# Query features and attention sums of the later groups: sixteen 32x32 tiles of TensorE, or four 64x64 tiles with a pair of heads in each

## The chip, the cores and the metric

One core of a Trainium2 chip runs the whole kernel. The metric is device time in microseconds (us), taken as the median of several runs. Beside it stands the profile of one execution.

## What is computed

A linear attention with polynomial features, followed by a two-layer feed-forward block with ELU, all in 32-bit floats:

```python
a = einsum('rd,bhsd->bhsr', S1, x); b = einsum('rd,bhsd->bhsr', S2, x)   # r = 8
phi(x) = outer(a, b)                          # 64 features
kv  = einsum('bhsf,bhsd->bhfd', phi(k), v);   z = phi(k).sum(over s)
num = einsum('bhsf,bhfd->bhsd', phi(q), kv)
den = einsum('bhsf,bhf->bhs', phi(q), z) + 1e-06
x   = (num / den) as 4352 tokens x 128        # 4 batches x 1088, 4 heads x 32
h   = x @ w_in                                # 128 -> 2048
out = where(h > 0, h, exp(min(h, 0)) - 1) @ w_out   # 2048 -> 128
```

## The kernel before, in words

**Groups and steps.** The 4352 tokens are 68 half tiles of 64 tokens (17 of each batch), taken in nine groups: eight of 512 tokens (8 half tiles) and a last one of 256. For each group the 2048 hidden channels are worked off in 8 pairs of 128 channels (`cp`). A pair of a group is a step; the list `steps` (L837) holds 72 of them: groups 0 and 1 share steps 0 to 15, then each group has eight steps in a row (2 from step 16, 3 from 24, 4 from 32 and so on).

**One step.** The loop at L925 writes out the order of every engine by hand; no planner reorders it. In step n TensorE makes h (`mm1`, records at L219) in two PSUM banks, then what `extra` holds for the step, then the second product of step n - 2: `o` for groups 0 and 1 (`mm2`, L219), `pa` and `pb` for groups 2 to 7 (`mm2_seven`, L668, seven products in place of eight, on sums `tt` that POOL makes), `ol` for the last group. ACT makes the exponential of h (L729, L731), DVE joins both into `gg` (L737), which lets go of the h bank. Four PSUM banks carry h, so a step's banks are those of the step two before. Two more banks have the tag `aux` and are shared by whatever comes up; the last two take o, pa and pb. The product of a step thus has two steps' time for ACT, DVE and POOL.

**Products in tiles.** TensorE is used in tiles. `halves` (L217) splits a product into two column halves (128x64 tiles). `KF_late` (L309), key features, uses eight 64x32 tiles. Every product of 32-bit floats shows as two records of TensorE, and two weight loads.

**Queries of the later groups.** Groups 2 to 8 get their x while the steps run. They are taken in units (L479): groups 2 and 3 alone, groups 4 and 5, 6 and 7 as pairs, and 8 alone. `un` is half of a unit's half tiles: 4, 4, 8, 8 and 2. For a unit the following happens, at the steps listed at L894:
- `q1` (L494) projects q with `SWq`, which holds for each batch and head the 32x32 block of S1, S2 and z (the last 8 columns are zero). It runs in sixteen 32x32 tiles: head h is the row of tiles, and c, a quarter of the unit's tokens, is the column. Head h writes bank h.
- `q1_out` (L504): four DVE transposes, one for each bank, put tokens on partitions (`abw`).
- `q2_den`, `q2_half` (L517, L572): division by the denominator and the outer product (DVE). `q4` (L580): DVE transposes features back onto partitions (`qpT`).
- `q5` (L587) multiplies with `kvq`, in two halves f of the features, again in sixteen 32x32 tiles: quarter c is the row of tiles and writes bank c, head h is the column.
- `q5_out` (L599): ACT copies x into `xg`, the input of mm1.

`parts` (L482) cuts a quarter where a batch ends inside it; the rest of the quarter then is a product of its own, and the products are sorted so that the rests come last. This occurs in units 2, 4 and 6.

`queries` (L609) runs at steps 13, 15, 22, 30, 46 and 62 and joins q5 of one unit with q1 of the next: q5 for f = 0, q1, q5 for f = 1. It takes four banks: the two h banks of the next step, ahead of that step's mm1, and both aux banks. x takes columns 0 to 255 of each, the features columns 256 to 511. q5_out and q1_out stand in the middle of the same step (`mid`), for a pair of groups the second q5_out at its end (`late`), so that mm1 of the next step can write the h banks.

**What feeds them.** `make_SWq` (L271, POOL, step 2) writes S1 and S2 into SWq for each batch, `Z_share` (L389, POOL) adds z of the batch when its keys are done, and `KV_out` (L399, DVE) copies the batch's sums from PSUM into kvq. `bmask` (L205) has a one for each channel at its head.

Of the kernel before, what the change touches and what calls it, by code (L numbers as in the profile page):

```python
# [12 lines left out]
F32 = mybir.dt.float32  # L13
# [9 lines left out]
def _ap(ap: bass.AP, free):  # L23
    return dataclasses.replace(ap, ap=[list(ap.ap[0])] + [list(x) for x in free])
# [3 lines left out]
def kernel(  # L28
# [21 lines left out]
    nc = tc.nc  # L50
    B, H, S, D = q.shape
    R = S1.shape[0]
    P = 128
    FD = H * D
# [9 lines left out]
    const = ctx.enter_context(tc.tile_pool(name="const", bufs=1))  # L64
    work = ctx.enter_context(tc.tile_pool(name="wk", bufs=2))
    psum = ctx.enter_context(tc.tile_pool(name="psum", bufs=2, space=bass.MemoryType.PSUM))
# [6 lines left out]
    qT = [const.tile([FD, NT, 64], F32, name=f"qT{b}") for b in range(2)] * 2  # L73
# [125 lines left out]
    for b in range(B):  # L199
        nc.gpsimd.memset(vt[b][64:, :VN].rearrange("p (h t d) -> p h t d", h=H, t=KT)[:, :, KT - 1, :], 0.0)  # L200
        if b < 2:
# [3 lines left out]
    bmask = const.tile([FD, H], F32, name="bmask")  # L205
# [2 lines left out]
    nc.vector.tensor_reduce(zmask[:].rearrange("p g i -> p (g i)"),  # L208
                            ident[:].rearrange("p (x j) -> p x j", j=R), axis=AX, op=ADD)

    hmask = const.tile([P, H], F32, name="hmask")
    nc.vector.tensor_reduce(hmask[:], _ap(zmask[:], [[1, H], [H, 4]]), axis=AX, op=ADD)

# [8 lines left out]
    def keep_warm(n, cols=256):  # L222
        for i in range(n):
            nc.tensor.matmul(idle[:, :cols], some[:, :P], some[:, :cols], skip_group_check=True)  # L224
# [26 lines left out]

    Sab = const.tile([FD, H, 2 * R], F32, name="Sab")
    SW = const.tile([FD, H, 3, R], F32, name="SW")
    SWq = const.tile([FD, B, 4, R], F32, name="SWq")
    keep_warm(3)
    keep_warm(1, 96)
    sps = psum.tile([P, 512], F32, name="sps", tag="aux")
# [7 lines left out]
    Sxp = const.tile([FD, 2, 2, R], F32, name="Sxp")  # L265
# [3 lines left out]
                             Sab[:, 2:].rearrange("p c (x r) -> p c x r", x=2))  # L269

    def make_SWq():  # L271
        nc.gpsimd.memset(SWq[:, :, 3, :], 0.0)
        for b in range(B):
            nc.gpsimd.tensor_add(SWq[:, b, :2, :], Sxp[:, :, 0, :], Sxp[:, :, 1, :])


    def outer(dst, ab, eng=nc.vector):
# [7 lines left out]
    kvq = const.tile([P, B, 2, H, D], F32, name="kvq")  # L285
# [102 lines left out]

    def Z_share(b):  # L389
        z = wzs.pop(b)  # L390
        zp = work.tile([FD, 2, R], F32, name="zp", tag="zp")
        nc.gpsimd.tensor_add(zp[:], z[:, :2], z[:, 2:])
        nc.gpsimd.tensor_add(SWq[:, b, 2, :], zp[:, 0], zp[:, 1])

    def KV(b, ps):
        for f in range(2):
            halves(ps[:, 128 + P * f:128 + P * f + P], kvz[b][:, f].rearrange("p c s -> p (c s)"), ident[:])

    def KV_out(b, ps):  # L399
        nc.vector.tensor_copy(kvq[:, b].rearrange("p f h d -> p (f h d)"), ps[:, 128:384])  # L400


    def Z_first():
# [14 lines left out]
    def KV_first():  # L418
        ps = psum.tile([P, 512], F32, name="kvps", tag="aux")
        KV(0, ps)  # L420
        KV_out(0, ps)
# [3 lines left out]
    NQ = (NH + 7) // 8  # L425
    qn = [min(8, NH - 8 * g) // 2 for g in range(NQ)]
    abw, ans, qp, qpT, xg, xps = {}, {}, {}, {}, {}, {}
# [4 lines left out]
    def half_tile(g, k):  # L432
        return divmod(8 * g + k, NT)
# [45 lines left out]
    units = {g: ([g, g + 1] if 4 <= g < NQ - 1 else [g]) for g in [2, 3] + list(range(4, NQ, 2))}  # L479
    un = {g: sum(qn[x] for x in gr) for g, gr in units.items()}  # L480

    def parts(g, c):  # L482

        n = un[g] // 2
        k = 0
        while k < n:
            b, t = half_tile(g, n * c + k)
            m = min(n - k, NT - t)
            yield b, t, k, m
            k += m  # L490

    def q1(g, ps, start=True):  # L494
        todo = [(j, c, h, x) for c in range(4) for h in range(H) for j, x in enumerate(parts(g, c))]
        for j, c, h, (b, t, k, m) in sorted(todo, key=lambda x: x[0]):
            r = slice(D * h, D * h + D)
            nc.tensor.matmul(ps[h][32 * c:32 * c + 32, 256 + 64 * k:256 + 64 * (k + m)],
                             SWq[r, b].rearrange("p x r -> p (x r)"),
                             qT[b][r, t:t + m, :].rearrange("p t s -> p (t s)"), start=start and j == 0, stop=True,  # L500
                             skip_group_check=True, tile_position=(D * h, 32 * c))
        abw[g] = ps

    def q1_out(g):  # L504
        ps, n = abw[g], un[g]
        pair = n > 4
        abw[g] = work.tile([P, H * n if pair else H * 4, 4 * R], F32, name="abw", tag="abwp" if pair else "abw",
                           bufs=1 if pair else 2)
        for h in range(H):
            nc.vector.transpose(abw[g][:, n * h:n * h + n, :].rearrange("p m y -> p (m y)"),  # L510
                                ps[h][:, 256:256 + 32 * n])

    def q2(g, parts=1):
        q2_den(g)
        q2_out(g, parts)
# [17 lines left out]
    def q2_out(g, parts=1):  # L533
        m = H * qn[g]
        x, an = abw.pop(g), ans.pop(g)
        qp[g] = work.tile([P, 4 * H, R, R], F32, name="qp", tag="qp", bufs=2)
        for i in range(parts):
            h = slice(i * m // parts, (i + 1) * m // parts)
            a_ = an[:, h]
            b_ = x[:, h, :R]  # L540
            nc.vector.tensor_mul(qp[g][:, h], _ap(a_, list(a_.ap[1:]) + [[0, R]]),  # L541
                                 _ap(b_, [b_.ap[1], [0, R], b_.ap[2]]))
# [26 lines left out]
    def heads(g):  # L569
        return 2 if un[g] > 4 else H  # L570
# [15 lines left out]

    def q5(g, ps, f):  # L587
        n = un[g]
        todo = [(j, h, c, x) for h in range(H) for c in range(4) for j, x in enumerate(parts(g, c))]
        for j, h, c, (b, t, k, m) in sorted(todo, key=lambda x: x[0]):  # L590
            i, o = divmod(h, heads(g))
            r = slice(32 * c, 32 * c + 32)
            nc.tensor.matmul(ps[c][D * h:D * h + D, 64 * k:64 * (k + m)], kvq[r, b, f, h, :],  # L593
                             qpT[g, i][r, n * o + 2 * k:n * o + 2 * (k + m), f, :],
                             start=(f == 0 and j == 0), stop=(f == 1),
                             skip_group_check=True, tile_position=(32 * c, D * h))
        xps[g] = ps

    def q5_out(g, i=0):  # L599

        ps, n, gr = xps[g], 32 * un[g], units[g]
        x = xg[g + i] = work.tile([P, 512], F32, name="xg", tag="xg", bufs=3)
        cs = range(4 // len(gr))
        for c in cs:

            o = n * c if g < NQ - 1 else n * (2 * (c % 2) + c // 2)
            nc.scalar.copy(x[:, o:o + n], ps[c + len(cs) * i][:, :n])

    def queries(g5, g1, n):  # L609

        hs[steps[n]] = [psum.tile([P, 512], F32, name="h", tag="h", bufs=4) for c in range(2)]
        ps = hs[steps[n]] + [psum.tile([P, 512], F32, name="qps", tag="aux") for _ in range(2)]

        if g5 is not None:
            q5(g5, ps, 0)
        if g1 is not None:
            q1(g1, ps, g5 is None)
        if g5 is not None:
            q5(g5, ps, 1)


    hs, es, gs, ops = {}, {}, {}, {}
# [214 lines left out]
    steps = [(0, 0), (0, 1), (1, 0), (1, 1)] + [(g, cp) for cp in range(2, NP) for g in range(2)]  # L837
# [19 lines left out]

    late(2, make_Sxp)
    late(2, make_SWq)
    late(3, Z_share, 0)  # L860
    late(3, KC, 0)
    late(8, KV_first)
# [10 lines left out]
    def turned(b):  # L873
        Z_out(b, kv_ps[b])
        KV_out(b, kv_ps[b])
        Z_share(b)
# [17 lines left out]
    for n, g, nx in ((13, None, 2), (15, 2, 3), (22, 3, 4), (30, 4, 6), (46, 6, 8), (62, 8, None)):  # L894
        at(n, queries, g, nx, n + 1)
        if g is not None:
            mid(n, q5_out, g)
        if nx is not None:
            mid(n, q1_out, nx)
        if g is not None and len(units[g]) > 1:  # L900
            late(n, q5_out, g, 1)
# [23 lines left out]
    for n in range(2, N + 2):  # L925
        if n < N:
            g, cp = steps[n]
# [26 lines left out]
        g, cp = steps[n - 2]  # L954
# [39 lines left out]
```

## Time and profile before

| | us |
|---|---|
| runs before, median of 5 | 269.46 |
| lowest and highest | 268.44 and 270.56 |
| the profiled execution | 270.49 |
| its span, first to last instruction | 268.7 |
| TensorE busy in the span | 262.3 |
| DVE, ACT, POOL busy | 189.7, 182.1, 166.0 |

The span is what the profile sees; the profiled execution's own time has some 1.8 us more around it. "PE" is TensorE's products and "PEld" its weight loads, which can lie beside them. A line such as `133.99 0.41 PE L593 MATMUL h<-qpT,kvq 32*32 32x128 f32 x2` in the timeline gives start and length in us, the line of the code, the tile written and those read, the rows and columns of the TensorE tile, rows by columns of the streamed operand, and how many records were merged. The recorded length of a product holds the way through the array (a 32x64 one has 0.22 us, a 32x256 one 0.39), so starts tell more than lengths. In the chain of what ended last, each line has start, length and the work that held the end at that time. In a table of stretches, each line has the bounds, the length, then the busy time of PE, PEld, DVE, ACT and POOL with numbers of instructions, the granted clock, the DMA share and GB/s.

### The profile page before, as it was taken

To read this page: it belongs to the slowest core of one execution; us is meant where nothing else is said; L and a number is where in the kernel's file an instruction comes from. 1 tells how busy PE (TensorE), PEld (TensorE's weight loads), DVE (VectorE), ACT (ScalarE), POOL (GpSimd) and SP (SyncE) were. 2 spreads that over 40 slices of the span, in tenths; PEclk is the share of its full clock that TensorE was granted. 3 is DMA by queue.
4 is the path that set the end of the run, shared out by engine and by line. 5 is a ranking of instruction groups with operands and counts; after the bars stand their busy time and mean duration, and the time that the engine had idled before them with its cause. 6 is when DMAs were issued, how large, how long until landed. Compare 5 with 4: busy or idle time off the path is not lost.

```text
span 268.7 us, 8155 instructions
## 1 busy us (share of the span) xinstructions
PE 262.3 (98%) x3343; PEld 157.0 (58%) x3343; DVE 189.7 (71%) x350; ACT 182.1 (68%) x351; POOL 166.0 (62%) x233
## 2 busy tenths in 40 slices
PE   8899999999999999999999999999999999999994
PEld 5853333343343666666676666666766666666884
DVE  6599999996969896997658667464347444673652
ACT  2368978685565656676667766777777767677782
POOL 4500006402506996699979999988698889897300
PEclk9999999999999999999999999999999999999999
DMA  6997882002001300000200110001001100110021
GB/s 190 310 348 197 233 223 47 0 2 83 2 2 29 53 4 2 2 2 11 31 7 0 16 27 2 2 11 23 10 4 15 28 1 2 17 16 12 2 29 32
DMA packets 26420, 13.63 MB, mean 51 GB/s; under 512 B 19216, under 2 KB 24592, under 8 KB 26384
## 3 DMA queue, kind: packets, MB, share of 16 engines
q1 hardware_dynamic: 25792, 12.66, 19.6%
q8 instruction: 26, 0.43, 0.7%
q10 hardware_dynamic: 592, 0.46, 0.5%
q14 instruction: 10, 0.08, 0.1%
HBM read 10.88 MB, written 2.23 MB: 49 GB/s over the span
## 4 chain that ended last, share of the span: by engine, by line
PE 88%; DVE 6%; POOL 2%; issue 1%; ACT 1%; DVEq 0%
PE h L219 40%; PE pb L668 15%; PE pa L668 12%; PE o L219 9%; PE ol L219 3%; PE h L593 2%; PE idle L224 2%; PE kv L365 1%; DVE gg L737 1%; DVE qp L541 1%; PE abp L296 1%; POOL kp L280 1%; PE kfps L315 1%; POOL tt L651 1%; PE kv L219 1%
## 5 line engine op out<-in xcount | busy, mean ns | idle before, releaser
L737 DVE SCALAR_TENSOR_TENSOR gg<-e,h 128x512 f32<-128x512 f32 (+1 forms) x144 | 92.3, 651 | 63.2 <-ACT e L731 58.4
L219 PE MATMUL h<-xg,W 128*64 128x512 f32 (+1 forms) x584 | 128.7, 563 | 0.0
L729 ACT ACTIVATE e<-h 128x512 f32<-128x512 f32 (+1 forms) x144 | 81.5, 566 | 56.0 <-PE h L219 55.1
L731 ACT ACTIVATE e<-e 128x512 f32<-128x512 f32 (+1 forms) x144 | 87.5, 607 | 4.4
L219 PEld LDWEIGHTS h<-xg,W 128*64 128x64 f32 x584 | 40.2, 137 | 47.3 <-issue 36.8
L651 POOL TENSOR_TENSOR tt<-gg 128x256 f32<-128x256 f32 x48 | 39.2, 818 | 11.1 <-DVE gg L737 10.7
L648 POOL TENSOR_TENSOR tt<-gg 128x256 f32<-128x256 f32 x48 | 35.1, 732 | 14.5 <-DVE gg L737 14.3
L653 POOL TENSOR_TENSOR tt<-gg,tt 128x256 f32<-128x256 f32 x48 | 38.5, 801 | 3.8
L652 POOL TENSOR_TENSOR tt<-tt,gg 128x256 f32<-128x256 f32 x48 | 36.0, 749 | 3.8
L668 PEld LDWEIGHTS pa<-gg,W 128*64 128x64 f32 x384 | 23.6, 137 | 22.6 <-issue 22.0
L219 PE MATMUL o<-gg,W 128*64 128x512 f32 x128 | 30.5, 597 | 0.4 <-DVE W L125 0.4
L668 PE MATMUL pa<-gg,W 128*64 128x128 f32 x384 | 29.5, 275 | 0.0
L668 PE MATMUL pb<-tt,SS 128*64 128x128 f32 x384 | 29.1, 273 | 0.0
L668 PEld LDWEIGHTS pb<-tt,SS 128*64 128x64 f32 x384 | 22.7, 137 | 0.0
L122 POOL TENSOR_TENSOR raw<-raw,tiny 128x512 f32<-128x512 f32 x1 | 1.0, 1042 | 29.6 <-DVE raw L117 29.6
L668 PE MATMUL pa<-tt,SS 128*64 128x128 f32 x192 | 18.7, 273 | 0.2 <-POOL tt L652 0.2
L668 PE MATMUL pb<-gg,SS 128*64 128x128 f32 x192 | 18.7, 273 | 0.0
L668 PE MATMUL pb<-tt,W 128*64 128x128 f32 x192 | 18.7, 273 | 0.0
L219 PEld LDWEIGHTS o<-gg,W 128*64 128x64 f32 x128 | 8.6, 137 | 15.8 <-issue 13.2
L668 PEld LDWEIGHTS pa<-tt,SS 128*64 128x64 f32 x192 | 12.1, 137 | 0.5 <-POOL tt L652 0.5
L668 PEld LDWEIGHTS pb<-gg,SS 128*64 128x64 f32 x192 | 12.1, 137 | 0.2 <-issue 0.2
L668 PEld LDWEIGHTS pb<-tt,W 128*64 128x64 f32 x192 | 12.2, 137 | 0.0
(137 smaller groups left out, 258.0 us busy)
## 6 DMA issues: line engine op xcount, KB each, us to landing
raw<-in_moe_w_in_dram SPq DMA_DIRECT2D x8, 256.0 KB, 6.0
raw<-in_moe_w_out_dram SPq DMA_DIRECT2D x8, 256.0 KB, 6.2
hd_k<-in_k_dram SPq DMA_DIRECT2D x3, 544.0 KB, 8.1
hd_q<-in_q_dram SPq DMA_DIRECT2D x3, 544.0 KB, 3.4
v<-in_v_dram SPq DMA_DIRECT2D x4, 288.0 KB, 7.0
out_dram<-ob SPq DMA_DIRECT2D x72, 16.0 KB, 1.5
v<-in_v_dram SPq DMA_DIRECT2D x4, 256.0 KB, 8.8
out_dram<-ob SPq DMA_DIRECT2D x16, 32.0 KB, 1.7
```

The source lines that it names most:

```text
L219: nc.tensor.matmul(dst[64 * u:64 * u + 64], lhs[:, 64 * u:64 * u + 64], rhs, skip_group_check=True, tile_position=(0, 64 * u), **kw)
L224: nc.tensor.matmul(idle[:, :cols], some[:, :P], some[:, :cols], skip_group_check=True)
L280: eng.tensor_mul(dst, _ap(a_, list(a_.ap[1:]) + [[0, R]]), _ap(b_, [b_.ap[1], [0, R], b_.ap[2]]))
L593: nc.tensor.matmul(ps[c][D * h:D * h + D, 64 * k:64 * (k + m)], kvq[r, b, f, h, :], qpT[g, i][r, n * o + 2 * k:n * o + 2 * (k + m), f, :], ...
L648: nc.gpsimd.tensor_tensor(t[:, 0], b12, b11, op=SUB)
L651: nc.gpsimd.tensor_tensor(t[:, 2], b22, b12, op=SUB)
L652: nc.gpsimd.tensor_tensor(t[:, 1], t[:, 2], b11, op=ADD)
L653: nc.gpsimd.tensor_tensor(t[:, 3], b21, t[:, 1], op=SUB)
L668: nc.tensor.matmul(bank[64 * u:64 * u + 64, P * col:P * col + P], lhs, rhs[:, u], start=(first and i in (0, 3)), stop=last, skip_group_che ...
L729: nc.scalar.activation(e, hs[g, cp][c][:, :n], RELU, scale=-1.0)
L731: nc.scalar.activation(e, e, EXP, scale=-1.0)
L737: nc.vector.scalar_tensor_tensor(gs[g, cp][:, c, :n], es[g, cp][:, c, :n], -1.0, hs[g, cp][c][:, :n], op0=ADD, op1=MAX)
```

## The change

Two neighbouring heads share a product: the stationary block has 64 rows (two heads of 32) and 64 columns, with zeros where head and column belong to different heads of the pair. Four 64x64 tiles take the place of sixteen 32x32 tiles, in q1 and in q5: a pair of heads r is one side, a half w of the unit's tokens (in place of quarters c) the other.

- SWq becomes 64 columns wide for a pair (`[FD, B, 2, 4, R]`); make_SWq writes copies of Sxp, which has the zeros already, and Z_share needs one addition instead of two.
- kvq gets zeros by a mask `cmask` (one new POOL instruction at the start): KV_out is a multiplication in place of a copy.
- q1 and q5 stream up to 512 columns per product. Over all six steps q1 has 26 products in place of 92, q5 has 52 in place of 184.
- q1_out has two transposes per unit, of twice the width, in place of four; q5_out one copy per group of a pair and two for a single group, in place of two and four.
- queries takes banks by need: where x and features fit side by side in 512 columns (steps 13, 15 and 62), both use the two aux banks alone, and mm1 of the next step gets its h banks as in any other step. Elsewhere (steps 22, 30 and 46) x takes one h bank and one aux bank, and the features the other two.

```diff
+    cmask = const.tile([P, 2], F32, name="cmask")
+    nc.gpsimd.tensor_add(cmask[:], bmask[:, :2], bmask[:, 2:])
...
-            nc.gpsimd.tensor_add(SWq[:, b, :2, :], Sxp[:, :, 0, :], Sxp[:, :, 1, :])
+            nc.gpsimd.tensor_copy(SWq[:, b, :, :2, :].rearrange("p c x r -> p x c r"), Sxp[:])
...
-        zp = work.tile([FD, 2, R], F32, name="zp", tag="zp")
-        nc.gpsimd.tensor_add(zp[:], z[:, :2], z[:, 2:])
-        nc.gpsimd.tensor_add(SWq[:, b, 2, :], zp[:, 0], zp[:, 1])
+        nc.gpsimd.tensor_add(SWq[:, b, :, 2, :], z[:, :2], z[:, 2:])
...
-        nc.vector.tensor_copy(kvq[:, b].rearrange("p f h d -> p (f h d)"), ps[:, 128:384])
+        nc.vector.tensor_mul(kvq[:, b].rearrange("p f (g c) d -> p (f g) c d", c=2),
+                             ps[:, 128:384].rearrange("p (x c d) -> p x c d", c=2, d=D),
+                             _ap(cmask[:], [[0, 4], [1, 2], [0, D]]))
...
-    def parts(g, c):
-        n = un[g] // 2
+    def parts(g, w):
+        n = un[g]
...
+    def q1(g, ps, start, o):
+        todo = [(j, w, r, x) for w in range(2) for r in range(2) for j, x in enumerate(parts(g, w))]
+        for j, w, r, (b, t, k, m) in sorted(todo, key=lambda x: x[0]):
+            rows = slice(64 * r, 64 * r + 64)
+            nc.tensor.matmul(ps[r][64 * w:64 * w + 64, o + 64 * k:o + 64 * (k + m)],
+                             SWq[rows, b].rearrange("p c x r -> p (c x r)"),
+                             qT[b][rows, t:t + m, :].rearrange("p t s -> p (t s)"), start=start and j == 0, stop=True,
+                             skip_group_check=True, tile_position=(64 * r, 64 * w))
...
-        for h in range(H):
-            nc.vector.transpose(abw[g][:, n * h:n * h + n, :].rearrange("p m y -> p (m y)"),
-                                ps[h][:, 256:256 + 32 * n])
+        for r in range(2):
+            nc.vector.transpose(abw[g][:, 2 * n * r:2 * n * r + 2 * n, :].rearrange("p m y -> p (m y)"),
+                                ps[r][:, o:o + 64 * n])
...
+        todo = [(j, w, r, x) for r in range(2) for w in range(2) for j, x in enumerate(parts(g, w))]
+            nc.tensor.matmul(ps[w][64 * r:64 * r + 64, 64 * k:64 * (k + m)],
+                             kvq[rows, b, f, 2 * r:2 * r + 2, :].rearrange("p c d -> p (c d)"),
+                             qpT[g, i][rows, o + 2 * k:o + 2 * (k + m), f, :],
+                             start=(f == 0 and j == 0), stop=(f == 1),
+                             skip_group_check=True, tile_position=(64 * w, 64 * r))
...
+        nx, nq = (64 * un[g] if g is not None else 0 for g in (g5, g1))
+        if nx + nq > 512:
+            hs[steps[n]] = [psum.tile([P, 512], F32, name="h", tag="h", bufs=4) for c in range(2)]
+        aux = [psum.tile([P, 512], F32, name="qps", tag="aux") for _ in range(2)]
+        if nx + nq > 512:
+            xb, qb, o = [hs[steps[n]][0], aux[0]], [hs[steps[n]][1], aux[1]], 0
+        else:
+            xb, qb, o = aux, aux, nx
```

More of the change, by code (lines that the diff above doesn't have):

```diff
@@ L253 @@
     SW = const.tile([FD, H, 3, R], F32, name="SW")
-    SWq = const.tile([FD, B, 4, R], F32, name="SWq")
+    SWq = const.tile([FD, B, 2, 4, R], F32, name="SWq")
     keep_warm(3)
@@ L271, in make_SWq @@
     def make_SWq():
-        nc.gpsimd.memset(SWq[:, :, 3, :], 0.0)
+        nc.gpsimd.memset(SWq[:, :, :, 3, :].rearrange("p b c r -> p (b c) r"), 0.0)
         for b in range(B):
-            nc.gpsimd.tensor_add(SWq[:, b, :2, :], Sxp[:, :, 0, :], Sxp[:, :, 1, :])
+            nc.gpsimd.tensor_copy(SWq[:, b, :, :2, :].rearrange("p c x r -> p x c r"), Sxp[:])
     def outer(dst, ab, eng=nc.vector):
@@ L480 @@
     un = {g: sum(qn[x] for x in gr) for g, gr in units.items()}
-    def parts(g, c):
-        n = un[g] // 2
+    def parts(g, w):
+        n = un[g]
         k = 0
         while k < n:
-            b, t = half_tile(g, n * c + k)
+            b, t = half_tile(g, n * w + k)
             m = min(n - k, NT - t)
@@ L490, in parts @@
             k += m
[L494 to L502, printed above, removed]
+    def q1(g, ps, start, o):
[6 more added lines that the diff above has]
+                             skip_group_check=True, tile_position=(64 * r, 64 * w))
+        abw[g] = ps, o
     def q1_out(g):
-        ps, n = abw[g], un[g]
+        (ps, o), n = abw[g], un[g]
         pair = n > 4
@@ L588, in q5 @@
         n = un[g]
[L589 to L594, printed above, removed]
+        todo = [(j, w, r, x) for r in range(2) for w in range(2) for j, x in enumerate(parts(g, w))]
@@ L595, in q5 @@
+        for j, w, r, (b, t, k, m) in sorted(todo, key=lambda x: x[0]):
+            i, o = (r, 0) if n > 4 else (0, 2 * n * r)
+            rows = slice(64 * w, 64 * w + 64)
+            nc.tensor.matmul(ps[w][64 * r:64 * r + 64, 64 * k:64 * (k + m)],
+                             kvq[rows, b, f, 2 * r:2 * r + 2, :].rearrange("p c d -> p (c d)"),
+                             qpT[g, i][rows, o + 2 * k:o + 2 * (k + m), f, :],
                              start=(f == 0 and j == 0), stop=(f == 1),
-                             skip_group_check=True, tile_position=(32 * c, D * h))
+                             skip_group_check=True, tile_position=(64 * w, 64 * r))
@@ L597, in q5 @@
         xps[g] = ps
     def q5_out(g, i=0):
-        ps, n, gr = xps[g], 32 * un[g], units[g]
+        ps, n = xps[g], 64 * un[g]
+        pair = len(units[g]) > 1
         x = xg[g + i] = work.tile([P, 512], F32, name="xg", tag="xg", bufs=3)
[L603 to L607, printed above, removed]
-    def queries(g5, g1, n):
-        hs[steps[n]] = [psum.tile([P, 512], F32, name="h", tag="h", bufs=4) for c in range(2)]
-        ps = hs[steps[n]] + [psum.tile([P, 512], F32, name="qps", tag="aux") for _ in range(2)]
+        for w in [i] if pair else range(2):
+            if pair:
+                to = x[:]
+            elif g < NQ - 1:
+                to = x[:, n * w:n * w + n]
+            else:
+                to = x[:, :2 * n].rearrange("p (k w s) -> p w k s", w=2, s=64)[:, w]
+            nc.scalar.copy(to, ps[w][:, :n] if g < NQ - 1 else ps[w][:, :n].rearrange("p (k s) -> p k s", s=64))
@@ L614, in queries @@
+    def queries(g5, g1, n):
+        nx, nq = (64 * un[g] if g is not None else 0 for g in (g5, g1))
[4 more added lines that the diff above has]
+            xb, qb, o = [hs[steps[n]][0], aux[0]], [hs[steps[n]][1], aux[1]], 0
+        else:
+            xb, qb, o = aux, aux, nx
         if g5 is not None:
-            q5(g5, ps, 0)
+            q5(g5, xb, 0)
@@ L616, in queries @@
         if g1 is not None:
-            q1(g1, ps, g5 is None)
+            q1(g1, qb, o == 0, o)
         if g5 is not None:
-            q5(g5, ps, 1)
+            q5(g5, xb, 1)
     hs, es, gs, ops = {}, {}, {}, {}
```

## The prediction

> **What bounds the kernel now.** I read the page's busy times first, then the chain that ended last, then the chain in order of time, and last the six stretches in which the products of the change run.
>
> ```profile
> PE 262.3 (98%) x3343; PEld 157.0 (58%) x3343; DVE 189.7 (71%) x350; ACT 182.1 (68%) x351; POOL 166.0 (62%) x233
> ...
> PEclk9999999999999999999999999999999999999999
> ...
> PE 88%; DVE 6%; POOL 2%; issue 1%; ACT 1%; DVEq 0%
> ```
>
> TensorE is busy 98% of the span, at the full granted clock, and 88% of the chain is its. From 24 us on it hardly ever stops. So a change counts by what it does to TensorE's own time, and work of other engines counts only where TensorE waits for it. A regular stretch of the chain shows the rhythm and the price of products in smaller tiles:
>
> ```profile
> 37.89 1.72 PE h L219 x8
> 39.61 0.65 PE kfps L315 x16
> 40.26 1.87 PE o L219 x8
> 42.12 1.72 PE h L219 x8
> ```
>
> Each product leaves two records (two passes). Eight records of h, in pairs of column halves that run side by side, take 1.72 us, so one pass of 512 columns takes 0.43 us: **0.84 ns a column**, whatever the number of tiles beside it. The step from h to h is 42.12 - 37.89 = 4.23 us; h and o alone would take 3.44, so the eight 64x32 tiles of kfps (L315), all side by side, cost 0.79. Their two passes of 288 columns are 2 x 288 x 0.84 ns = 0.48. The other **0.31 us** is the way into another tile shape and back (o takes 1.87 in place of 1.72 behind it).
>
> The six stretches from the end of h to the next product of the main work:
>
> ```profile
> 66.75:67.44 0.69, 0.69 (x43) 0.47 (x41) 0.04 (x1) 0.69 (x2) 0.61 (x2) 1.00 0.00 0
> 74.36:76.40 2.04, 1.96 (x114) 1.53 (x112) 2.04 (x3) 0.61 (x1) 0.00 (x0) 1.00 0.00 0
> 103.38:105.17 1.79, 1.79 (x107) 1.31 (x105) 0.69 (x1) 0.61 (x1) 1.63 (x3) 1.00 0.03 9
> 133.89:136.38 2.49, 2.49 (x122) 1.92 (x120) 0.69 (x1) 0.62 (x1) 2.33 (x4) 1.00 0.11 19
> 188.36:190.36 2.00, 2.00 (x114) 1.61 (x113) 0.69 (x1) 0.62 (x1) 1.84 (x4) 1.00 0.12 16
> 242.33:243.22 0.89, 0.89 (x67) 0.67 (x65) 0.18 (x1) 0.62 (x1) 0.78 (x2) 1.00 0.22 31
> ```
>
> The first number is the length. Measured from h to h less a regular step (3.44 us with o, 3.24 us with pa and pb: 144.45 - 141.21 in the timeline), they cost 0.73, 2.09, 1.85, 2.55, 2.06 and 0.94: **10.2 us** in all, 4% of the span. That is all that the change can touch on TensorE.
>
> Why do they cost so much? Sixteen tiles side by side stream a quarter of the columns each; step 30 (the fourth) would need 3 waves x 2 passes x 256 columns x 0.84 ns = 1.29 us. Its start and a later part:
>
> ```profile
> 133.99 0.41 PE L593 MATMUL h<-qpT,kvq 32*32 32x128 f32 x2
> 134.00 0.41 PE L593 MATMUL qps<-qpT,kvq 32*32 32x256 f32 x2
> 134.01 0.41 PE L593 MATMUL h<-qpT,kvq 32*32 32x128 f32 x2
> ...
> 134.31 0.39 PE L593 MATMUL h<-qpT,kvq 32*32 32x128 f32 x2
> ...
> 134.41 0.54 PE L593 MATMUL h<-qpT,kvq 32*32 32x128 f32 x5
> 134.68 0.36 PE L498 MATMUL h<-qT,SWq 32*32 32x192 f32 x2
> ```
>
> The first sixteen records start within 0.1 us; the tails behind a batch boundary (x2 at 134.31, x5 at 134.41) hold the next wave until 134.68; then they start some 15 ns apart (pairs at 134.68, 134.71, 134.74 in the timeline). 120 records in 2.4 us is one every 20 ns: the old form is bound by **the issue of many small products**, not by streaming.
>
> **What the change does to TensorE.** It removes 198 of 276 products (q1 92 to 26, q5 184 to 52), and doubles what each tile streams, since half of each stationary block is zero. If the four 64x64 tiles run side by side, a step costs 0.31 plus its longest tile's columns x 2 passes x 0.84 ns:
> - step 13, q1 of 256 columns: 0.43 + 0.31 = 0.74 against 0.73
> - step 15, 3 x 256: 1.29 + 0.31 = 1.60 against 2.09
> - step 22, 256 + 512 + 256: 1.72 + 0.31 = 2.03 against 1.85
> - step 30, 3 x 512: 2.58 + 0.31 = 2.89 against 2.55
> - step 46, 512 + 128 + 512: 1.94 + 0.31 = 2.25 against 2.06
> - step 62, 2 x 128: 0.43 + 0.31 = 0.74 against 0.94
>
> The sum is 10.25 against 10.2: **+0.05 us**. The long steps lose what the short ones gain: one limit takes the place of another. Step 15 holds 0.37 us that is not streaming: its first products begin at 74.45, the rest at 74.83, when gg (L737, 74.12 for 0.65 us) has let go of the second h bank. The new form keeps both parts in the two aux banks there, so this wait goes; next late is qpT (L584, ends at 74.20), which is still in time.
>
> **The other engines.** q5_out of step 22 becomes two ACT copies of 256 columns instead of four of 128. Four end 0.82 us behind the last product (105.99), two take 0.65 (two at 136.49): the next exp, and the gg behind it, come 0.12 earlier. This matters, since q2, kp and gg are then queued on DVE up to the one stall that TensorE has later: the eight pa records from 114.95 stream until 115.39 (a pair of 128 columns each 0.11 us), and the next, which waits for tt (L652), comes at 115.80. These 0.41 us should shrink by 0.12. q1_out becomes two transposes where four were (L510, 0.41 each for 256 columns; 512 take 0.71 at L694): 1.4 us either way, and no more behind ACT's copies where the banks differ. Its cover is the 1.5 us of pa and pb before h writes the banks; without it each 0.1 us would show.
>
> KV_out's copy (0.42) becomes a product with a mask: 0.42 by cc (L691, 128x256 too), at most 0.77 by an (L530, 128x256 with a broadcast operand); I take the first, which also reads a PSUM bank. DVE idles 1.7 us behind the first (65.27), and around the last one tt is ready 1.4 us or more ahead of its product (126.61 in the timeline, where it is read after 128.05). Z_share loses one of two POOL adds (0.22); q1 comes 0.9 us behind it anyway (65.93 to 66.85). make_SWq's adds become copies (0.22 each; a copy of 128x64 took 0.24 at L262), after which POOL idles for 30 us. cmask is one POOL instruction of some 0.2 us ahead of idr (done at 3.05), which TensorE reads at 4.86. All these cost nothing. No DMA moves.
>
> **Sum:** 0.05 - 0.12 = -0.07 us. Against the profiled execution (270.49, of which 268.7 is span) that is 270.4; the median of the runs lies 1.03 below it, so I forecast **269.4 us**, no change.
>
> The unknown is whether four 64x64 tiles pack. The trace has no such tile. Below, its bounds are the full packing of kfps; above, the prices of the rivals. I take the packing, since kfps with 64x32 is the nearest row.
>
> One rule speaks against it. The Trainium skill, "TensorE: Matmul & The Clock Gate", section "Part 3: Packing small matmuls — row/col tiling", says that a weight load overlaps running products only where the row group differs; here two tiles share each row group, and every tile follows itself. The rows of h disagree: its halves use all 128 rows, their loads (0.14 us) lie in the 0.43 us of the products before. By the rule 42 passes would pay 0.14 us each, an estimate of +5.9 us; by the rows nothing.
>
> **Rivals.**
> - *Tails in line* (slower): a wave split at a batch boundary (q1 of 2, 4, 6; q5 of 2, 4, 6, twice each) has two tails, on different tiles. If the second starts only once the first is in its second pass, one pass of a tail is lost each time: 192 columns in three waves, 384 in three, 320 in three, together 2688 x 0.84 ns = 2.26 us, so **271.7**. For it: the tails at 134.31 to 134.68. Against: those came 17th in the queue, where the start-up burst ends in unsplit waves too; the new steps 15 and 46 have 16 products in all. It decides a "slower" from 0.6 of its price.
> - *Loads in the open*: the first pass behind a change of shape pays some 0.05 us (o 40.19 to 40.67, 0.48 for 0.43). The longest tiles of the six steps have 4, 10, 8, 12, 10 and 4 passes, 48 less the first of each: if all these pay, 42 x 0.05 = 2.1 us: **271.5**. Against: h pays it once.
> - *It does not pack*: only two of four tiles stream at once. The streams, 8.4 us, double: **277.8**. Against: kfps.
> - *More gain*: the entry price falls to kfps's bare gap of about 0.2 (0.10 in, 0.09 out) and the stall at 115.80 closes: -0.07 - 6 x 0.11 - 0.28 = -1.0: **268.4**. For it: a 64x64 burst is in the queue before it starts.
>
> **How the numbers follow.** Chances: forecast 0.60, tails 0.17, loads 0.07, no packing 0.04, more gain 0.12. 0.5% is 1.35 us, about what a measurement here tells from no change (the runs before spread over 0.8%). Beyond it lie half of "more gain" and a little of the forecast's scatter on the fast side (0.09), and most of tails and loads and all of no packing on the slow side (0.23); 0.68 lies within. The range, 268.1 to 271.7, leaves out no packing, half of the tails and a part of "more gain".
>
> **What the new profile would show.** Right: the six stretches near 0.7, 1.5, 2.0, 2.8, 2.2 and 0.7 us, no break at step 15, pairs of 64*64 records of 512 columns 0.43 us apart on a tile. Tails: gaps of 0.2 to 0.3 us inside steps 15, 30 and 46. No packing: step 30 near 5.5 us. If a stall at h behind queries appears (L219 waiting for abw or xg), I have misjudged the cover.

## The result and the profile after

| | before | after |
|---|---|---|
| median, us | 270.56 (77 runs) | 270.51 (40 runs) |
| lowest and highest | 268.42 to 271.82 | 268.32 to 271.06 |
| the profiled execution; its span | 270.49; 268.7 | 270.98; 269.2 |
| span from the first o to the end | 244.74 | 244.75 |

The ratio after to before is 0.9995, with a 95% interval of 0.9981 to 1.001: **no change**, and the interval allows at most 0.2% either way. That is what was forecast. The forecast time, 269.4, is 1.1 us off, and the five runs of before that it started from (median 269.46) were as much off from the 77 (270.56). The last row is the sharpest comparison: behind the first o nothing of the start plays in, and the two kernels differ by 0.01 us.

The page after, busy times and the line of the chain (shares of the span):

```profile
PE 263.0 (98%) x2947; PEld 156.3 (58%) x2947; DVE 188.6 (70%) x340; ACT 181.5 (67%) x341; POOL 165.2 (61%) x230
...
PE 92%; DVE 4%; POOL 1%; ACT 1%; issue 1%; DVEq 0%
```

396 records of TensorE are gone (two for each of 198 products), and its busy time is 0.7 us longer. Of this, 0.52 us lie ahead of the first o (21.91 against 21.39 us busy there); the part on the start shows that they aren't the change's.

The rhythm of the main work, in the chain in order of time:

```profile
38.40 1.72 PE h L222 x8
40.12 0.65 PE kfps L318 x16
40.76 1.87 PE o L222 x8
42.63 1.71 PE h L222 x7
```

42.63 - 38.40 is 4.23 us, as before. What the change does to TensorE is therefore in the six stretches (bounds, length, busy PE, PEld, DVE, ACT, POOL with their numbers of instructions, granted clock, DMA share, GB/s):

```profile
67.26:67.95 0.69, 0.69 (x14) 0.31 (x12) 0.04 (x1) 0.69 (x2) 0.61 (x2) 1.00 0.00 0
74.87:76.44 1.57, 1.57 (x35) 1.05 (x33) 1.57 (x3) 0.62 (x1) 0.00 (x0) 1.00 0.00 0
103.41:105.39 1.98, 1.98 (x31) 1.11 (x29) 0.98 (x2) 0.61 (x1) 1.82 (x4) 1.00 0.00 0
134.04:136.87 2.83, 2.83 (x38) 1.70 (x36) 1.41 (x3) 0.61 (x1) 2.67 (x5) 1.00 0.04 6
188.85:191.04 2.19, 2.19 (x34) 1.42 (x32) 1.21 (x3) 0.61 (x1) 2.03 (x4) 1.00 0.10 15
243.04:243.73 0.69, 0.69 (x18) 0.42 (x16) 0.00 (x0) 0.60 (x1) 0.61 (x2) 1.00 0.16 24
```

The predicted terms (0.74, 1.60, 2.03, 2.89, 2.25, 0.74) held the 0.05 us that the next product pays; less that they are 0.69, 1.55, 1.98, 2.84, 2.20, 0.69. The largest miss is 0.02. The sum is 9.95 against 9.90 before: +0.05, as predicted.

How the tiles pack is seen in step 30, on TensorE (start, length, line, operation, tile, merged records):

```profile
134.13 0.32 PE L598 MATMUL h<-qpT,kvq 64*64 64x128 f32 x1
134.14 0.64 PE L598 MATMUL qps<-qpT,kvq 64*64 64x512 f32 x1
...
134.29 0.60 PE L598 MATMUL h<-qpT,kvq 64*64 64x128 f32 x4
134.62 0.60 PE L598 MATMUL qps<-qpT,kvq 64*64 64x512 f32 x2
134.73 0.50 PE L598 MATMUL h<-qpT,kvq 64*64 64x384 f32 x2
135.05 0.32 PE L503 MATMUL h<-qT,SWq 64*64 64x192 f32 x1
135.06 0.59 PE L503 MATMUL h<-qT,SWq 64*64 64x512 f32 x1
...
135.91 0.59 PE L598 MATMUL qps<-qpT,kvq 64*64 64x512 f32 x1
```

A wave that is split at a batch boundary writes 128 columns, then the other 384, to the tiles of h, while the tiles of qps stream 512 at once. The second passes of 384 run from 134.73, beside those of 512 (134.62). The next wave begins at 135.05 and the last at 135.91, 0.86 us on: two passes of 512 columns at 0.84 ns. No tile is held up by another's rest.

The one later stall, that before pa's second half:

```profile
115.18 0.61 PE L684 MATMUL pa<-gg,W 128*64 128x128 f32 x8
115.94 0.44 PE L684 MATMUL pa<-tt,SS 128*64 128x128 f32 x4 [0.16 <-POOL tt L668]
```

The eight stream for 0.44 us (0.11 a pair), so the stall is 115.94 - 115.18 - 0.44 = 0.32 us; it was 0.41.

### The profile page after: what moved, and what is told of

The parts are those of the page before. It is cut to its first block, busy times and chain, and to the rows that moved or that the text cites. A ratio compares the mean times of both kernels' runs of the same rounds, so it can differ in the third digit from the quotient of the medians.

```text
span 269.2 us, 7341 instructions
## 1 busy us (share of the span) xinstructions
PE 263.0 (98%) x2947; PEld 156.3 (58%) x2947; DVE 188.6 (70%) x340; ACT 181.5 (67%) x341; POOL 165.2 (61%) x230
## 4 chain that ended last, share of the span: by engine, by line
PE 92%; DVE 4%; POOL 1%; ACT 1%; issue 1%; DVEq 0%
PE h L222 41%; PE pb L684 15%; PE pa L684 12%; PE o L222 11%; PE ol L222 3%; PE idle L227 2%; PE kv L368 1%; PE qps L598 1%; PE h L598 1%; PE abp L299 1%; DVE qp L546 1%; PE kfps L318 1%; PE h L503 1%; POOL tt L667 1%; PE kv L222 1%
```

## The start, and why the runs lie on two levels

The runs of both kernels leave a gap: none of before's 77 lies between 269.88 and 270.24, none of after's 40 between 269.67 and 270.20. Below it lie 23 and 12 runs, with medians 268.80 and 268.53; above it medians 270.74 and 270.73. The change moves neither the levels nor the shares (30% of the runs lie below the gap in both). What differs between profiled executions is the start. Three views of TensorE, of before, of after, and of e7 below:

```profile
9.18 0.24 PE L296 MATMUL abp<-Sab,kT 128*64 128x64 f32 x1
...
9.29 0.65 PE L450 MATMUL abqp<-Sab,qT 128*64 128x64 f32 x13
```

```profile
9.18 0.32 PE L299 MATMUL abp<-Sab,kT 128*64 128x64 f32 x1
...
9.34 1.11 PE L453 MATMUL abqp<-Sab,qT 128*64 128x64 f32 x13
```

```profile
5.71 1.67 PE L299 MATMUL abp<-Sab,kT 128*64 128x64 f32 x36
7.37 0.69 PE L453 MATMUL abqp<-Sab,qT 128*64 128x64 f32 x16
```

Products of 64 columns take 0.32 us at first and 0.22 to 0.24 later, as if TensorE's clock became full in between. The trace's record of the granted clock begins with full at such a moment: at 9.20 us before, at 10.46 after, and at 4.33 in e7. The same kernel does not repeat it: after once more (e8) has it at 9.77. The first o and the end follow:

| clock full at | kernel | first o | from there to the end | its time |
|---|---|---|---|---|
| 4.33 | e7 | 22.01 | 244.86 | 268.66 |
| 9.20 | before | 23.94 | 244.74 | 270.49 |
| 9.77 | e8, after again | 24.19 | 244.75 | 270.73 |
| 10.46 | after | 24.45 | 244.75 | 270.98 |

All of the 0.49 us between the two profiled executions is there (24.45 - 23.94 = 0.51). That the whole lower level is made of early clocks is inferred from e7, the only profiled execution on it that does the kernel's full work (e2, below, took 269.75 us with a clock full at 9.33, but its steady part is 0.76 us shorter). An early clock doesn't suffice: e6 has it at 4.28, but waits 0.97 us for q's transpose, and reaches o at 23.16.

## Experiments

Stretches are those of the six steps, in us. The theory: the new form is bound by its streams plus 0.31 us a step, the old one by the issue of small products, and at step 15 by a wait for a bank; that the two sums are equal is chance. The main rival: the old form is as fast as it can be, and rests behind batch boundaries, or loads, eat the new form's gain. The second half (e9 to e11) is about the wait alone.

**e1: banks of h at every step.**

```diff
-        if nx + nq > 512:
+        if True:
```

> The new form, with the h banks of the next step taken at every query step (13, 15 and 62 too), instead of the two aux banks alone. Theory (the gain of step 15 is the wait for gg that the aux banks spare): the stretch of step 15 grows from 1.57 to 1.9 us or more, with a break of 0.3 to 0.4 us behind its first products until gg has let go of the h bank; steps 13 and 62 stay at 0.69 and 0.71. Rival (step 15 gained because it has fewer products): it stays at 1.57 us.

Measured 270.96 us (one run; before 270.67): stretches 0.69, 1.57, 1.98, 2.83, 2.19, 0.69. Step 15 did not grow; the expectation missed. In this layout x uses only the bank of h that comes free first; the features use the second, and they stream 0.5 us later.

**e2 and e3: no split at batch boundaries**, in the old form and in the new. The tokens behind a boundary are then taken from the first batch.

```diff
-            m = min(n - k, NT - t)
-            yield b, t, k, m
+            m = n
+            yield b, min(t, NT - n), k, m
```

> The old form with every quarter as one product: where a batch ends inside it, the tokens are taken from the first batch alone, so those tokens' outputs are not the reference's. q1 has 80 products instead of 92, q5 160 instead of 184. Theory (the old form is bound by the issue of many small products, some 16 ns each): steps 15, 30 and 46 lose only the share of products that go, a fifth at most, so 2.49 becomes 2.1 to 2.3 us in step 30. Rival (the old form is bound by the rests behind the batch boundaries, which stand in line): each split wave falls from 0.7 to about 0.45 us, so step 30 falls from 2.49 to 1.7 us and step 46 from 2.00 to 1.4.

> The new form with every half as one product, in the same way (outputs of the tokens behind a boundary are not the reference's). q1 has 20 products instead of 26, q5 40 instead of 52. Theory (the new form is bound by its streams, the rests fill their tile at no cost): the six stretches stay within 0.05 us of 0.69, 1.57, 1.98, 2.83, 2.19 and 0.71. Rival (rests cost in line here too): steps 30 and 46 fall by 0.3 us or more.

Measured 269.75 (old) and 270.70 (new; one run each, before 270.67). The old form's stretches:

```profile
66.80:67.32 0.52, 0.52 (x34) 0.23 (x32) 0.00 (x0) 0.52 (x2) 0.44 (x2) 1.00 0.00 0
74.24:76.29 2.05, 1.95 (x99) 1.25 (x97) 2.05 (x4) 0.62 (x1) 0.00 (x0) 1.00 0.00 0
103.26:104.98 1.72, 1.72 (x98) 1.25 (x96) 0.69 (x1) 0.61 (x1) 1.56 (x3) 1.00 0.03 10
133.69:135.85 2.16, 2.16 (x99) 1.31 (x97) 0.69 (x1) 0.62 (x1) 2.08 (x3) 1.00 0.09 15
187.82:189.65 1.83, 1.83 (x98) 1.12 (x96) 0.69 (x1) 0.62 (x1) 1.67 (x4) 1.00 0.18 28
241.63:242.51 0.88, 0.88 (x67) 0.66 (x65) 0.18 (x1) 0.61 (x1) 0.76 (x2) 1.00 0.12 18
```

9.16 in place of 9.90: the old form pays 0.74 us for its rests. The new form's stretches are 0.69, 1.55, 1.98, 2.83, 2.19, 0.69, 9.93 in place of 9.95: its rests are free, and *tails in line* falls. The last row is telling: step 62 has no split, and its two waves need only 2 x 2 passes x 64 columns x 0.84 ns = 0.22 us of streaming; with the price of shape (0.31 less the 0.05 behind the stretch) that is 0.48. It takes 0.88: 0.20 us more for each wave of 16 small products. The same sum for steps 22, 30 and 46 (three waves; 0.86, 1.29 and 0.97 us of streaming) gives 0.20 a wave each time; only step 13, a single wave, has 0.04. What the 0.20 consist of isn't settled, but the trace of e2 shows where they lie. The first passes of the single wave start 7 ns apart, like those of the first wave in step 30. There the second wave begins at 134.25 and 134.44, with nothing started between, and goes on with a product every 17 ns. Only two of its weight loads (134.03 and 134.25) begin before 134.43. Whether the queue of products or the loads hold it, no run separates. Step 15 keeps its break.

**e4: a mixture**, units 4 and 6 (long streams) in the old form, with an unmasked copy of kvq for them, the others in the new.

```diff
+            if g5 is not None:
+                q5_old(g5, ps, f) if o5 else q5(g5, ps, f)
```

> Units 2, 3 and 8 in the new form, the pairs of groups (units 4 and 6) in the old one, with a second, unmasked copy of the sums for these (three more DVE copies of 0.42 us). Step 22 has q5 new and q1 old, step 46 q5 old and q1 new. Theory (the new form wins where streams are short, loses where they are long): step 30 back at 2.49, steps 13, 15 and 62 at 0.69, 1.57 and 0.71; steps 22 and 46 pay two more changes of tile shape, 1.9 to 2.1 us each. Sum 9.4 to 9.6 us, so 0.3 to 0.5 us less than before over the same stretches, 0.1 to 0.2% of the time: within what the timing can tell. Rival (changes of shape cost 0.3 us each): steps 22 and 46 at 2.3 us or more and no gain.

Measured: median 270.45 (12 runs) against 270.67 (17), ratio 0.9988, interval 0.9966 to 1.001: no change that the runs can tell. Stretches 0.69, 1.56, 2.08, 2.50, 2.27, 0.69, sum 9.79, from the first o 244.56: 0.18 us less than before, where 0.3 to 0.5 were expected. Steps 22 and 46 hold one unit of each form, change the shape of tiles twice more, and take 2.08 and 2.27, longer than either pure form (1.79 or 1.98; 2.00 or 2.19).

**e5: the other bank.** The banks of h are taken at step 15 (in the code n is 16 there), as in e1, with x in the tile named second.

```diff
+            if n == 16:
+                xb, qb = qb, xb
```

> The new form, at step 15 alone with x of half 0 in the second h bank (and the features in the first); with h banks but x in the first one, step 15 had kept its 1.57 us. Theory (step 15 of the old form waits for the gg that lets go of the second h bank, and the new form escapes since nothing but the features, streamed later, can lie there): the products of half 0 now start only when gg (L753) of step 14 has ended. By the run before, gg ends some 0.13 us behind h there, 0.41 in the old form, so the break is 0.05 to 0.1 us and the stretch 1.6 to 1.7. Rival (the old form's break at step 15 has another cause): half 0 starts 0.10 us behind h as before, 1.57 us.

Measured 270.54 (one run, before 270.46); step 15 took 1.57, no break; a miss. The reason came out with e9 and e11 below.

**e6: the old form with its rests in place**, not sorted to the end (q5 is shown; q1 is changed in the same way).

```diff
-        for j, h, c, (b, t, k, m) in sorted(todo, key=lambda x: x[0]):
+        for j, h, c, (b, t, k, m) in todo:
```

> The old form with the rest behind a batch boundary issued right behind its quarter's first product, not at the end of the wave. Theory (a rest costs the old form 0.1 us a wave because it comes in line behind sixteen others): the split waves lose most of that, steps 13, 30 and 46 fall to 0.55, 2.2 and 1.85 us. Rival (a rest waits for its own tile and holds all that is queued behind it): the three steps grow, 30 to 2.6 us or more.

Measured 270.66 (one run, before 270.46); stretches 0.89, 1.94, 2.02, 2.70, 2.64, 0.88, sum 11.07, from the first o 245.72, 0.98 us more than before. The start, with its early clock, hides most of this in the time. The rival's times were right, and sorting was worth 1.2 us of stretches in the old form. Its reason holds only in part, as the first wave of step 30 shows:

```profile
133.35 0.41 PE L593 MATMUL h<-qpT,kvq 32*32 32x128 f32 x2
...
133.44 0.41 PE L593 MATMUL qps<-qpT,kvq 32*32 32x256 f32 x2
...
133.70 0.57 PE L593 MATMUL h<-qpT,kvq 32*32 32x128 f32 x6
134.01 0.41 PE L593 MATMUL qps<-qpT,kvq 32*32 32x256 f32 x2
```

The first rest, second in the kernel's order, starts at 133.60, when its tile is free. Thirteen of the sixteen quarters start between 133.35 and 133.46 all the same, twelve of them behind a waiting rest. Only the last three, behind the fourth rest, come late, at 133.89 to 134.03. So a rest doesn't hold the next product; what makes the queue stop behind the fourth isn't shown.

**e7: narrow copies in the new form**, four transposes and four ACT copies as in the old one.

```diff
-                nc.vector.transpose(abw[g][:, 2 * n * r:2 * n * r + 2 * n, :].rearrange("p m y -> p (m y)"),
-                                ps[r][:, o:o + 64 * n])
+            for y in range(2):
+                m = 2 * n * r + n * y
+                nc.vector.transpose(abw[g][:, m:m + n, :].rearrange("p m y -> p (m y)"),
+                                    ps[r][:, o + 32 * n * y:o + 32 * n * y + 32 * n])
```

> The new form with the old widths of the copies: four DVE transposes per unit instead of two, and two ACT copies where one was (four for a single group). Theory (the narrower copies delay exp and gg behind step 22, and so the tt that TensorE waits for near 116 us): the stall there grows from 0.33 back to about 0.40 us, the six stretches stay, and from the first o to the end it takes 244.8 instead of 244.75 us. Rival (the stall is POOL's own): it stays at 0.33.

Measured 268.66 (one run, early clock; before 270.46). Stretches as after; the stall before pa's second half:

```profile
112.73 0.61 PE L690 MATMUL pa<-gg,W 128*64 128x128 f32 x8
113.64 0.44 PE L690 MATMUL pa<-tt,SS 128*64 128x128 f32 x4 [0.29 <-POOL tt L674]
```

113.64 - 112.73 - 0.44 = 0.47, against 0.32 after (0.40 was expected): the wide copies are worth 0.15 us there, and 0.11 from the first o to the end. The width that counts is ACT's: in both runs the gg behind step 22 waits 0.95 us for ACT's exponential, after DVE's transposes have ended.

**e8: after once more**, unchanged.

> The changed kernel once more, nothing altered. Theory (0.5 us between the two profiles lie before the first o and come from the moment at which TensorE's clock rises, which is not the kernel's): first o as after the earlier moments, some 0.4 us later for each us by which the clock rises later (23.94 us at 9.20, 24.45 at 10.46), and 244.7 to 244.8 us from there to the end. Rival (the change itself costs 0.5 us at the start): first o at 24.4 us whenever the clock rises.

Measured 270.73; clock full at 9.77, first o at 24.19, 244.75 from there. The theory of the start held.

**e9 and e10: DVE late, without and with its control.** The first transposes are made twice, so that DVE comes to qpT and gg 0.7 us later; e9 has also the exchange of e5.

```diff
+            for _ in range(2 if g == 2 else 1):
+                nc.vector.transpose(abw[g][:, 2 * n * r:2 * n * r + 2 * n, :].rearrange("p m y -> p (m y)"),
+                                    ps[r][:, o:o + 64 * n])
```

> The new form with half of x of step 15 in the second bank of h, as in e5, and with the two transposes of the first features (q1_out of unit 2) made twice, so that DVE reaches qpT and the gg behind it about 0.72 us later (in e5 qpT ended near 73.94, gg let go of the second bank near 74.48, h ended at 74.41). Theory: the first products of x wait for gg, which lets go at about 75.20; they start near 75.25 and the stretch is about 2.3 us in place of 1.57. Rival (the old kernel's break at step 15 had another cause than this bank): they wait only for qpT, at about 74.65, and the stretch is about 1.8 us.

> The control: the new form as it is, x of step 15 in the aux banks, with the same transposes made twice. Both theories: the products of x wait for qpT alone, some 0.2 us behind the end of h, and the stretch of step 15 is about 1.8 us. If it is 2.3 here as well, the wait of e9 is not one for the bank.

Measured 271.44 and 270.94 (one run each, before 270.86); step 15 took 2.11 and 2.09. Both wait for qpT, and longer than expected: in e10 it ends 0.47 us behind h, not 0.24 as reckoned, and the products start 0.15 us behind it. e9 is like its control, so by its own text the wait for the bank was refuted. But x did not lie in the bank that it was meant to wait for: in the trace of e9 its products start at 75.42, while the gg that was to let go of that bank runs until 75.84. The reading on which e11 was built, and which its result bears out, is that a bank is given to whichever tile is written first, not to the tile named first. By it e9, like e5, had not moved anything, and x still had the bank that comes free early.

**e11: x in both banks of h, DVE late.** The banks of h are taken at step 15 as in e5, and the transposes are doubled as in e10.

```diff
+            if n == 16:
+                xb, qb = hs[steps[n]], aux
```

> The new form with x of step 15 in both banks of h and the features in the aux banks, and with the doubled transposes of e10 so that the gg behind qpT ends about 1 us behind h. A bank goes to whichever tile is written first, so e5 and e9 had only exchanged names: their half of x still lay in the bank that the earlier gg lets go of, and their wait was for qpT, as in e10. Here the first product of x takes the first bank and the second product (the other half of the tokens) must take the second one. Theory (the old kernel's break at step 15 is the wait for that second bank): the first product starts when qpT is done, the second about 0.4 to 0.5 us later, when gg has ended, all others behind it; the stretch of step 15 is 2.45 to 2.6 us (e10: 2.09). Rival (another cause): no break inside, 2.1 us.

Measured 272.04 (one run, before 270.99); stretch of step 15:

```profile
74.97:77.51 2.54, 1.92 (x34) 1.37 (x32) 2.54 (x4) 0.61 (x1) 0.00 (x0) 1.00 0.00 0
```

DVE and then TensorE within it:

```profile
74.19 1.24 DVE L590 STREAM_TRANSPOSE qpT<-qp 128x1024 f32<-128x1024 f32 x1
75.35 0.65 DVE L756 SCALAR_TENSOR_TENSOR gg<-e,h 128x512 f32<-128x512 f32 x1
75.92 1.30 DVE L241 STREAM_TRANSPOSE kT<-hd_k 128x1088 f32<-128x1088 f32 x1
```

```profile
75.57 0.30 PE L599 MATMUL h<-qpT,kvq 64*64 64x64 f32 x2 [0.43 <-DVE qpT L590]
76.05 0.66 PE L599 MATMUL h<-qpT,kvq 64*64 64x256 f32 x10 [0.18 <-DVE gg L756]
```

One product (two records) goes as soon as qpT is there, the next waits until gg has ended (76.00), and everything behind it waits too. This is the old kernel's picture at step 15 (two records at 74.45 and 74.53, the next at 74.83, behind a gg that ended at 74.77), made at will by the layout alone; 2.54 lies in the expected 2.45 to 2.6, and the control has 2.09.

## Why the prediction was right, and where it was wrong

- **The level (wrong; the step that failed).** "The median of the runs lies 1.03 below it, so I forecast 269.4": this took a median of five runs for the level of the kernel. The five were 268.44, 268.54, 269.46, 270.49 and 270.56; they straddle the gap, and three of them happened to lie below it, where only 30% of the 77 do. With 77 runs the median is 270.56, 0.07 *above* the profiled execution, not 1.03 below. The sum itself, 270.4 from the profiled 270.49, was 0.1 from the median measured; that it came so close owes something to luck, since the executions of that kernel lie between 268.42 and 271.82. The lowest and highest of the five runs stood 2.1 us apart and showed that something was there; the prediction read it as scatter.
- **What bounds the kernel** (right). Nothing off TensorE showed: the mask product takes 414 ns, the copies of SWq 224, and no stall at an h behind queries appeared.
- **Streams plus 0.31 us a step** (right, all six within 0.02). *It does not pack* and *loads in the open* fall with it: any exposed 0.05 us a pass would have given step 30 another 0.55 us.
- **The rule on weight loads.** In the Trainium skill, "TensorE: Matmul & The Clock Gate", section "Part 3: Packing small matmuls — row/col tiling", a load overlaps only with products of other row groups, though the same section also lets one go ahead into a background buffer. Here two tiles share each row group and 36 loads, 1.70 us of busy time, lie in step 30 (2.83) without lengthening it. The measurement decides against the rule on row groups; the rule's estimate, +5.9 us, did not come.
- **The old form is bound by issue, "not by streaming"** (right only in part). In e2 step 30 falls from 2.49 to 2.16, and the six stretches by 0.74, without a split. So its 2.49 us are 1.29 of streaming, 0.26 for the tile shape, 0.33 for rests and 0.61 for its three waves of small products (0.20 each, as in all steps but 13): streaming is half of it, and that the 0.20 are issue is not shown. The sum didn't use this; it took the old stretches as measured. The new form gains where the old tiles streamed little (step 62, -0.20) or waited (step 15, -0.47), and loses where they streamed 256 columns (steps 22, 30, 46: +0.19, +0.34, +0.19). The gain went there: from one limit to another.
- **The wait at step 15** (right; shown by e11, after e1, e5 and e9 had failed to touch it). After has no wait for the bank, since x lies in the aux banks; "next late is qpT" is seen in e10, which waits for it alone.
- **ACT's copies, 0.12 us at the stall** (right in kind; size 0.09). e7 gives 0.15 for the width itself. But the first copy now starts 0.12 us behind the end of the stretch (105.51 - 105.39) where it was 0.05 (105.22 - 105.17), probably since the stretch now ends on longer products; this takes back 0.07. The gg that follows starts 2.03 us behind the stretch before, 1.97 after and 2.09 in e7.
- **Sum.** Forecast 0.05 - 0.12 = -0.07; measured +0.05 - 0.09 = -0.04 from these terms, +0.01 from the first o to the end, a difference at the rounding of the stretches.
- **Rivals.** *Tails in line* falls with e3. *More gain* too: 0.31 us a step stayed, and the stall closed by 0.09, not by 0.40 (0.12 and the 0.28 more).

## What to carry to other kernels

Fewer, larger tile products pay only where the small ones were bound by their number or by a wait; work out both limits for each step (columns streamed per tile, and waves of small products times their price) before changing the form, since padding with zeros doubles the first while it divides the second. Take the level of a kernel from many runs, or compare two profiled executions from the first instruction of the steady part: here that part agreed to 0.01 us between three executions, while whole runs lay 2 us apart. Where an experiment is to move a buffer, look at which bank the compiler gave before believing a null result.

## What was not expected of the hardware

- TensorE's clock became full at 4.3 us or between 9.1 and 10.7 us after the start in the thirteen profiled executions, and the first o moved with it, between 22.0 and 24.6 us (23.16 in e6, which also waited for q's transpose). The page's row of the granted clock, in 40 slices, shows 9 from the first slice on in all of them; the lengths of equal records show it (0.32 us, then 0.22).
- Two more changes of tile shape inside a step made it longer than either pure form: 2.27 us against 2.00 and 2.19 (step 46 of e4).
- A product that waits for its own tile let those behind it go ahead, up to a point: in e6 quarters started 0.2 us before a rest that stands ahead of them, and still unsorted rests cost 1.2 us of stretches.
